# A DiT block on one core: computing the MLP scale on VectorE from transposed weight columns instead of in one TensorE section

## The chip, the cores and the metric

The kernel runs on one NeuronCore of a Trainium2 chip. The metric is the device time of one execution in microseconds (us), taken from repeated executions. A *median* below is over all runs of a kernel in one comparison; each comparison ran the kernel before in turn with the others on the same chip. The records also give the mean clock that TensorE was granted, as a share of full speed.

## The reference

One diffusion transformer block: B = 2 images, N = 256 tokens, D = 1152 channels, two heads, F = 4608 hidden units, all in bfloat16.

```python
mod = (_silu(c) @ w_mod).reshape(B, 6, 1, D)
shift_a, scale_a, gate_a, shift_m, scale_m, gate_m = [mod[:, i] for i in range(6)]
h = _layernorm(x) * (1 + scale_a) + shift_a
q, k, v = ...                       # from h @ wqkv
attn = _softmax(einsum('bqhd,bkhd->bhqk', q, k) * Dh ** -0.5)
a = einsum('bhqk,bkhd->bqhd', attn, v).reshape(B, N, D) @ wo
x = x + gate_a * a
h2 = _layernorm(x) * (1 + scale_m) + shift_m
return x + gate_m * (_gelu(h2 @ w_fc1) @ w_fc2)
```

The change concerns `scale_m`: 1152 numbers for each of two images, from a matrix product with only two rows.

## The kernel before

The activations are kept transposed (channels on partitions), so `scale_m` and `shift_m` are wanted as columns, [128 partitions, 9 chunks, image]. A section is made by 36 narrow matmuls: for each of nine k chunks, four column tiles of the array work on four interleaved quarters of the outputs, and a VectorE 32x32 transpose turns the result into columns.

```python
def vec_section(stat, w, name):                 # 9 x 4 matmuls of 288 columns
    pn = aux_tile([P, CTW], "pn")
    for k in range(KD):
        wk4 = w[:, k, :].rearrange("p (j q r) -> p q j r", q=4, r=32)
        for i in range(4):
            nc.tensor.matmul(pn[32 * i:32 * i + SW, :]..., stat[:, k, :], wk4[:, i, :, :],
                             start=(k == 0), stop=(k == KD - 1), tile_position=(0, 32 * i))
    dst = act.tile([P, KD, 32], FP32, name=name)
    nc.vector.transpose(dst..., pn[:])
    return dst
```

The MLP's gate already goes another way late in the kernel: its weights are loaded transposed, and VectorE multiplies each column block with a broadcast copy of silu(c) and sums along the free axis.

```python
def dot_section(wT, s_all, spill, dst):
    for j in range(KD):
        for b in range(B):
            nc.vector.scalar_tensor_tensor(spill, wT[:, j, :], 1.0, s_all[:, b, :], op0=ALU.mult, op1=ALU.mult,
                                           accum_out=dst[:, b * KD + j:b * KD + j + 1])
```

All weights and the activation transposes are issued by SyncE in program order, into one queue. This is that order in the middle of the kernel:

```python
w_v = load_panels("w_v", wqkv_v, 2 * D)          # 3 x 0.88 MB
load_section("w_gate_a", S_GATE_A, w_gate_a)     # 2.65 MB each
w_o = load_panels("w_o", wo_v, 0)
w_shift_m = load_section("w_shift_m", S_SHIFT_M)
# ... q, scores, softmax; attn_transpose(0), attn_transpose(1); value matmuls, attention gate ...
w_scale_m = load_section("w_scale_m", S_SCALE_M)
w_f1[0] = load_panels("w_f1_0", wfc1_v, 0)
# ... attention product, w_o groups of tiles 0 and 1 with LN2 statistics between ...
ln2_transpose(0)                                 # hT[:, :, tile] <- transposed xn2
# ...
ln2_transpose(1)
# two panels of w_f1_1
shift_m = vec_section(sT, w_shift_m, "shift_m")
scale_m = vec_section(sT, w_scale_m, "scale_m")
# w_o groups of tiles 2 and 3; between them, on ScalarE:
ln2_modulate(0, range(6)); ln2_modulate(0, range(6, KD))    # hT = hT * scale_m + shift_m, nine times
# fc1, first half of the tokens: matmul k needs modulation k
```

## Time and profile before

| | before |
|---|---|
| time, median of 3 runs | 244.07 us (244.01 to 244.39) |
| TensorE busy | 237.0 us of a span of 242.9 us |
| VectorE, ScalarE, GpSimd busy | 84.3, 66.0, 31.4 us |
| hT of the first half landed | 94.27 us |
| TensorE reaches fc1 | 98.72 us, without a gap |

TensorE is the bound, so only its own work and its gaps count. This is the order of time on SyncE in the kernel before (start, length, instruction, x count); the length is how long the issue held SyncE, not the transfer:

```profile
44.25 10.23 SPq L121 DMA_DIRECT2D w_o<-in_wo_dram  x3
54.58 4.64 SPq L115 DMA_DIRECT2D w_shift_m<-in_w_mod_dram  x3
```

By 59 us everything that the attention half needs has been issued, and w_shift_m with it; w_o went out at 44 us.

### The profile page before, as it was taken

What the parts mean: (1) busy time and instruction counts of PE and PEld (TensorE: products, weight loads), DVE (VectorE), ACT (ScalarE), POOL (GpSimd) and SP (SyncE); (2) the same over time, 40 slices, a digit from 0 to 9 for tenths busy, and PEclk for the clock granted to TensorE, in tenths of its full rate; (3) what the DMA queues carried; (4) which work ended last, traced back from release to release, by engine and by line L of the source; (5) the groups of instructions that cost most, each with busy time, mean ns of one, the idle gap of its engine ahead of it and who ended that gap; (6) DMA issues with size and microseconds to landing.
All of it is one profiled execution on the core that took longest, in us unless ns stands there. A gap on an engine that the chain in (4) does not pass through costs nothing.

```text
span 242.9 us, 3965 instructions
## 1 busy us (share of the span) xinstructions
PE 237.0 (98%) x1679; PEld 141.6 (58%) x1679; DVE 84.3 (35%) x195; ACT 66.0 (27%) x131; POOL 31.4 (13%) x47
## 2 busy tenths in 40 slices
PE   8999999999999999999999999999999999999994
PEld 2586444465666676888644444444665665656673
DVE  3762460315634776720000089993010000000001
ACT  6442250333614074774222223332000000000000
POOL 1000004000310515300000000003121111111111
PEclk9999999999999999999999999999999999999999
DMA  6999999999999998699999999996920000000000
GB/s 238 327 333 361 382 349 313 372 354 343 342 185 362 343 217 216 172 186 327 328 336 191 244 305 327 327 326 196 305 81 16 19 16 16 16 26 26 17 19 16
DMA packets 69757, 53.89 MB, mean 222 GB/s; under 512 B 19035, under 2 KB 64363, under 8 KB 69739
## 3 DMA queue, kind: packets, MB, share of 16 engines
q1 hardware_dynamic: 69008, 52.43, 74.8%
q0 software_dynamic: 704, 1.20, 1.7%
q8 instruction: 13, 0.21, 0.4%
q14 instruction: 5, 0.04, 0.1%
q10 hardware_dynamic: 27, 0.00, 0.0%
HBM read 48.08 MB, written 1.19 MB: 203 GB/s over the span
## 4 chain that ended last, share of the span: by engine, by line
PE 86%; SPq 7%; DMA 5%; issue 0%; DVE 0%; DVEq 0%
PE pacc L803 29%; PE pacc L742 29%; PE pacc L644 7%; PE pacc L535 7%; DMA w_shift_a<-in_w_mod_dram 5%; PE pacc L462 5%; SPq L109 4%; PE pacc L470 2%; SPq L115 2%; PE pa L562 1%; PE ps_s L490 1%; PE pn L388 1%; PE pk L298 1%; SPq L104 1%; PE pg L422 0%
## 5 line engine op out<-in xcount | busy, mean ns | idle before, releaser
L803 PE MATMUL pacc<-w_f,gT 128*128 128x384 bf16 (+2 forms) x468 | 70.5, 314 | 0.0
L742 PE MATMUL pacc<-hT,w_f 128*128 128x512 bf16 (+1 forms) x414 | 70.3, 333 | 0.0
L803 PEld LDWEIGHTS <-gT 128*128 128x128 bf16 x468 | 44.4, 98 | 26.3
L742 PEld LDWEIGHTS <-w_f 128*128 128x128 bf16 x414 | 40.5, 98 | 29.4
L453 DVE SCALAR_TENSOR_TENSOR late<-w_gate_mT,late 128x1152 bf16<-128x1152 bf16 x18 | 24.4, 1357 | 31.8 <-DMA w_gate_mT<-in_w_mod_dram 31.2
L809 DVE TENSOR_TENSOR tmp<-pacc,gate 128x384 f32<-128x384 f32 (+2 forms) x13 | 6.9, 527 | 66.9 <-PE pacc L803 54.8
L780 ACT ACTIVATE gT<-pacc 128x512 bf16<-128x512 f32 x26 | 15.5, 597 | 35.0 <-PE pacc L742 35.0
L811 POOL TENSOR_TENSOR o_sb<-tmp,x 128x384 bf16<-128x384 f32 (+1 forms) x12 | 11.7, 972 | 52.2 <-DVE tmp L809 52.2
L644 PE MATMUL pacc<-w_o,big 128*128 128x384 bf16 (+2 forms) x117 | 18.1, 314 | 0.0
L535 PE MATMUL pacc<-w_v,hT 128*128 128x384 bf16 x108 | 17.9, 326 | 0.0
L644 PEld LDWEIGHTS <-big 128*128 128x128 bf16 x117 | 10.9, 98 | 7.1 <-DVE big L286 0.6
L535 PEld LDWEIGHTS <-hT 128*128 128x128 bf16 x108 | 10.4, 98 | 7.2 <-issue 0.5
L269 PE MATMUL pk<-big,w_k 128*128 128x128 bf16 (+2 forms) x102 | 13.4, 278 | 0.0
L650 POOL TENSOR_TENSOR x<-tmp,x_sb 128x384 f32<-128x384 f32 (+1 forms) x11 | 9.8, 889 | 17.0 <-DVE tmp L649 10.6
L462 PE MATMUL pacc<-hT,w_q 128*128 128x512 bf16 x54 | 11.8, 379 | 0.0
L444 POOL DMA_DIRECT2D gates_dram<-grow x4 | 2.0, 513 | 66.3 <-DVE grow L766 66.3
L269 PEld LDWEIGHTS <-w_k 128*128 128x128 bf16 x102 | 7.8, 98 | 2.9
L462 PEld LDWEIGHTS <-w_q 128*128 128x128 bf16 x54 | 5.3, 98 | 6.4
L152 PE MATMUL pwarm<-zeros 128*128 128x512 bf16 x20 | 7.6, 553 | 1.2 <-DVE eps_t L92 1.2
L649 DVE TENSOR_TENSOR tmp<-pacc,gate 128x384 f32<-128x384 f32 (+2 forms) x13 | 6.7, 524 | 5.4 <-PE pacc L644 4.1
L627 ACT ACTIVATE hT<-hT,shift_m,scale_m 128x256 bf16<-128x256 bf16 x12 | 6.2, 587 | 5.0 <-DMA hT<-xn 5.0
L758 ACT ACTIVATE gT<-pacc 128x512 bf16<-128x512 f32 x10 | 5.6, 593 | 6.2 <-PE pacc L742 6.2
(98 smaller groups left out, 155.9 us busy)
## 6 DMA issues: line engine op xcount, KB each, us to landing
w_f<-in_w_fc_dram SPq DMA_DIRECT2D x14, 864.0 KB, 10.1
w_f<-in_w_fc_dram SPq DMA_DIRECT2D x2, 2592.0 KB, 11.9
w_f<-in_w_fc_dram SPq DMA_DIRECT2D x2, 1728.0 KB, 12.2
w_shift_a<-in_w_mod_dram SPq DMA_DIRECT2D x3, 864.0 KB, 11.7
w_v<-in_wqkv_dram SPq DMA_DIRECT2D x3, 864.0 KB, 11.3
w_gate_a<-in_w_mod_dram SPq DMA_DIRECT2D x3, 864.0 KB, 9.8
w_o<-in_wo_dram SPq DMA_DIRECT2D x3, 864.0 KB, 13.3
w_shift_m<-in_w_mod_dram SPq DMA_DIRECT2D x3, 864.0 KB, 9.7
```

What stands on the lines that cost most here:

```text
L109: nc.sync.dma_start(w_k[:, k, 0:KM1 * P], wqkv_v[:, k, D:D + KM1 * P])
L152: nc.tensor.matmul(dst[:], zeros[:, 0:P], zeros[:], start=True, stop=True)
L269: nc.tensor.matmul(pk[m][:, c0:c1], w_k[:, k, m * P:(m + 1) * P], hT0[:, k, c0:c1], start=(k == 0 and c0 == 0), stop=(k == KD - 1), skip_g ...
L453: nc.vector.scalar_tensor_tensor(spill, wT[:, j, :], 1.0, s_all[:, b, :], op0=ALU.mult, op1=ALU.mult, accum_out=dst[:, b * KD + j:b * KD + ...
L462: nc.tensor.matmul(pq[m][:], w_q[:, k, m * P:(m + 1) * P], hT[:, k, :], start=(k == 0), stop=(k == KD - 1),)
L535: nc.tensor.matmul(pacc[:], hT[:, k, t * P:(t + 1) * P], w_v[:, k, pnl * PW:(pnl + 1) * PW], start=(k == 0), stop=(k == KD - 1),)
L644: nc.tensor.matmul(pacc[:], aT[:, k, t * P:(t + 1) * P], w_o[:, k, c0:c1], start=(k == 0), stop=(k == KD - 1),)
L650: (nc.vector if (t, i) in ((1, 2), (3, 3)) else nc.gpsimd).tensor_tensor(x1[:, t, c0:c1], tmp[:], x_sb[:, t, c0:c1], op=ALU.add)
L742: nc.tensor.matmul(dst, w_f1[m // KD][:, k, ml * P:(ml + 1) * P], hT[:, k, c0:c1], start=(k == 0), stop=(k == KD - 1),)
L780: nc.scalar.activation(gT[:, m, :], pacc[:], ACT.Gelu_apprx_tanh)
L803: nc.tensor.matmul(pacc[:], gT[:, kk, t * P:(t + 1) * P], w_f2[j][:, r, c0 - n * PW:c0 - n * PW + cw], start=(kk == 0), stop=(kk == KF - 1),)
L811: (nc.vector if last else nc.gpsimd).tensor_tensor(o_sb[:], tmp[:], x1[:, t, c0:c0 + cw], op=ALU.add)
```

## The change

The intent is to take most of the scale section off TensorE. Two thirds of `scale_m` (six of nine column blocks) are computed by VectorE passes as for the MLP's gate, from weights loaded transposed; the last third by 36 matmuls of 96 columns straight after the attention gate's. For this the broadcast of silu(c) is made earlier, VectorE gives its q and value evictions to ScalarE, and the loads get a new order: the two transposed loads go among the value panels, and **w_o and w_shift_m move behind both attention transposes**.

```diff
@@ loads @@
+    w_scale_m = wide_tile("w_scale_m")
+    w_v = wide_tile("w_v")
     w_gate_a = wide_tile("w_gate_a")
-    w_v = load_panels("w_v", wqkv_v, 2 * D)
-    load_section("w_gate_a", S_GATE_A, w_gate_a)
-    w_o = load_panels("w_o", wo_v, 0)
-    w_shift_m = load_section("w_shift_m", S_SHIFT_M)
+    NDOT = 2 * CPP                                  # CPP = 3 blocks of 128
+    w_scale_mT = w_scale_m[:, 0:NDOT, :]
+    w_scale_mN = w_scale_m[:, NDOT:KD, :]...        # the plain third
+    def load_scale_mT(j):
+        c0 = S_SCALE_M * D + j * P
+        nc.sync.dma_start_transpose(w_scale_mT[:, j:j + CPP, :], w_mod[:, c0:c0 + PW])
@@ gate_natural: 32 weight columns, one eviction on ScalarE @@
-                    pn[32 * i:32 * i + B, :], sT[:, k, 0:B], wg[:, k, i * CTW:(i + 1) * CTW],
+                    pn[32 * i:32 * i + SW, :], sT[:, k, :], wg[:, k, i * CTW:(i + 1) * CTW],
@@ ahead of the q matmuls @@
+    for b in range(B):
+        nc.sync.dma_start(s_b[b][:], s_dram[b:b + 1, :].partition_broadcast(P))
+    load_scale_mT(0)
+    load_v(0)
+    load_section("w_gate_a", S_GATE_A, w_gate_a)
+    nc.sync.dma_start(w_scale_mN, wmod_v[:, :, S_SCALE_M * D + NDOT * P:(S_SCALE_M + 1) * D])
+    load_v(1)
+    load_scale_mT(CPP)
+    load_v(2)
+    scale_m_dots(0, CPP)                            # 6 VectorE passes
@@ q and value evictions @@
-        evac(...)                                   # VectorE and ScalarE in turn
+        nc.scalar.mul(...) / nc.scalar.copy(...)
@@ value loop @@
         if i == 1:
             gate_a = gate_natural(0, w_gate_a)
-
-    w_scale_m = load_section("w_scale_m", S_SCALE_M)
+            scale_mN = vec_section(sT, w_scale_mN, "scale_mN", KD - NDOT)
+        if i == 2:
+            scale_m_dots(CPP, NDOT)                 # 6 VectorE passes
+            ... add 1.0 to both parts
+    w_o = load_panels("w_o", wo_v, 0)
+    w_shift_m = load_section("w_shift_m", S_SHIFT_M)
     w_f1[0] = load_panels("w_f1_0", wfc1_v, 0)
@@ ahead of the third tile's w_o groups @@
     shift_m = vec_section(sT, w_shift_m, "shift_m")
-    scale_m = vec_section(sT, w_scale_m, "scale_m")
```

More of the change, by code (lines that the diff above doesn't have):

```diff
@@ L128, with load_v @@
     nc.sync.dma_start(w_q[:, :, KM1 * P:D], wqkv_v[:, :, KM1 * P:D])
+    w_scale_m = wide_tile("w_scale_m")
+    w_v = wide_tile("w_v")
     w_gate_a = wide_tile("w_gate_a")
-    w_v = load_panels("w_v", wqkv_v, 2 * D)
-    load_section("w_gate_a", S_GATE_A, w_gate_a)
-    w_o = load_panels("w_o", wo_v, 0)
-    w_shift_m = load_section("w_shift_m", S_SHIFT_M)
+    NDOT = 2 * CPP
+    w_scale_mT = w_scale_m[:, 0:NDOT, :]
+    w_scale_mN = w_scale_m[:, NDOT:KD, :].rearrange("p k n -> p (k n)").rearrange("p (k n) -> p k n", k=KD)
+    def load_scale_mT(j):
+        c0 = S_SCALE_M * D + j * P
+        nc.sync.dma_start_transpose(w_scale_mT[:, j:j + CPP, :], w_mod[:, c0:c0 + PW])
+    def load_v(n):
+        nc.sync.dma_start(w_v[:, :, n * PW:(n + 1) * PW], wqkv_v[:, :, 2 * D + n * PW:2 * D + (n + 1) * PW])
     big1 = act.tile([P, 4 * KD, T], BF16, name="big1", tag="big")
@@ L301, in k_panel, with store_by_quadrant @@
             )
+    s_dram = tc.dram_tile([B, D], BF16, name="s_dram")
+    def store_by_quadrant(dst, src, rows):
+        for a in range(4):
+            nc.gpsimd.dma_start(dst[a], src[32 * a:32 * a + rows])
+    s_rows = work.tile([P, KD, SW], BF16, name="s_rows", tag="s_rows", bufs=1)
     CUT = 4 * P
@@ L360 @@
     norm1(3, CUT, D, "d")
+    nc.vector.transpose(s_rows[:].rearrange("p k c -> p (k c)"), sT[:].rearrange("p k c -> p (k c)"))
+    store_by_quadrant(s_dram[:].rearrange("b (k a r) -> a b k r", a=4, r=32), s_rows, B)
     k_step(0, N + P, T)
@@ L381, with vec_section @@
     CTW = D // 4
-    def vec_section(stat, w, name):
-        pn = aux_tile([P, CTW], "pn")
+    def vec_section(stat, w, name, nk=KD):
+        pn = aux_tile([P, nk * 32], "pn")
         for k in range(KD):
@@ L392, in vec_section @@
                 )
-        dst = act.tile([P, KD, 32], FP32, name=name)
+        dst = act.tile([P, nk, 32], FP32, name=name)
         nc.vector.transpose(dst[:].rearrange("p k c -> p (k c)"), pn[:])
@@ L426, in gate_natural @@
         nat = work.tile([P, CTW], BF16, name="nat", tag="nat", bufs=1)
+        nc.scalar.copy(nat[:], pn[:])
         for i in range(4):
             rows = slice(32 * i, 32 * i + B)
-            if i % 2 == 0:
-                nc.vector.tensor_copy(nat[rows, :], pn[rows, :])
-            else:
-                nc.scalar.copy(nat[rows, :], pn[rows, :])
             nc.gpsimd.dma_start(gates_dram[g, :, i * CTW:(i + 1) * CTW], nat[rows, :])
@@ L437, in gate_natural, with dot_passes, scale_m_dots @@
         return gate
-    s_dram = tc.dram_tile([B, D], BF16, name="s_dram")
-    def store_by_quadrant(dst, src, rows):
-        for a in range(4):
-            nc.gpsimd.dma_start(dst[a], src[32 * a:32 * a + rows])
-    s_rows = work.tile([P, KD, SW], BF16, name="s_rows", tag="s_rows", bufs=1)
-    nc.vector.transpose(s_rows[:].rearrange("p k c -> p (k c)"), sT[:].rearrange("p k c -> p (k c)"))
-    store_by_quadrant(s_dram[:].rearrange("b (k a r) -> a b k r", a=4, r=32), s_rows, B)
-    def dot_section(wT, s_all, spill, dst):
-        for j in range(KD):
+    def dot_passes(wT, s_b, spill, dst, js):
+        for j in js:
             for b in range(B):
                 nc.vector.scalar_tensor_tensor(
-                    spill, wT[:, j, :], 1.0, s_all[:, b, :], op0=ALU.mult, op1=ALU.mult,
-                    accum_out=dst[:, b * KD + j:b * KD + j + 1],
-                )
-    gate_a = None
+                    spill, wT[:, j, :], 1.0, s_b[b], op0=ALU.mult, op1=ALU.mult, accum_out=dst(j, b),
+                )
+    s_b = [work.tile([P, D], BF16, name="s_b", tag="xn", bufs=4) for _ in range(B)]
+    s_spill = work.tile([P, D], BF16, name="s_spill", tag="xn", bufs=4)
+    for b in range(B):
[7 more added lines that the diff above has]
+    load_v(2)
+    scale_m = act.tile([P, KD, B], FP32, name="scale_m")
+    def scale_m_dots(j0, j1):
+        dot_passes(
+            w_scale_mT, [t[:] for t in s_b], s_spill[:], lambda j, b: scale_m[:, j, b:b + 1], range(j0, j1),
+        )
+    scale_m_dots(0, CPP)
     pq = [acc_tile([P, T], "pacc") for _ in range(KM1)]
@@ L473 @@
                 )
-        evac(qT[:, m, :], pq[m][:], attn_scale)
+        nc.scalar.mul(qT[:, m, :], pq[m][:], attn_scale)
     n_s = B * H * TPB
@@ L538, in v_group @@
             )
-        evac(v_sb[:, t, pnl * PW:(pnl + 1) * PW], pacc[:])
+        nc.scalar.copy(v_sb[:, t, pnl * PW:(pnl + 1) * PW], pacc[:])
     gate_a = None
@@ L550 @@
             gate_a = gate_natural(0, w_gate_a)
-    w_scale_m = load_section("w_scale_m", S_SCALE_M)
+            scale_mN = vec_section(sT, w_scale_mN, "scale_mN", KD - NDOT)
+        if i == 2:
+            scale_m_dots(CPP, NDOT)
+            nc.vector.tensor_scalar_add(scale_m[:, 0:NDOT, :], scale_m[:, 0:NDOT, :], 1.0)
+            nc.vector.tensor_scalar_add(scale_m[:, NDOT:KD, :], scale_mN[:, :, 0:B], 1.0)
+    w_o = load_panels("w_o", wo_v, 0)
+    w_shift_m = load_section("w_shift_m", S_SHIFT_M)
     w_f1 = [None] * 4
@@ L619, in ln2_transpose @@
         nc.sync.dma_start_transpose(hT[:, :, t * P:(t + 1) * P], xn2[t][:])
-    shift_m = scale_m = None
     def ln2_modulate(b, ks=range(KD)):
@@ L683 @@
     shift_m = vec_section(sT, w_shift_m, "shift_m")
-    scale_m = vec_section(sT, w_scale_m, "scale_m")
-    nc.vector.tensor_scalar_add(scale_m[:, :, 0:B], scale_m[:, :, 0:B], 1.0)
     wo_group(2, 0)
@@ L781 @@
         if m == 14:
-            dot_section(w_gate_mT, s_all, late[:, B, :], gcol)
+            dot_passes(
+                w_gate_mT, [s_all[:, b, :] for b in range(B)], late[:, B, :],
+                lambda j, b: gcol[:, b * KD + j:b * KD + j + 1], range(KD),
+            )
             gate_m = gate_m_finish()
```

## The prediction

> **What bounds the kernel now.** I read the page's shares, then the chain that ended last, then the order of time on each engine around the two places that the change touches (36 to 80 us and 86 to 100 us), then the DMA rates in short windows.
>
> ```profile
> PE 237.0 (98%) x1679; PEld 141.6 (58%) x1679; DVE 84.3 (35%) x195; ACT 66.0 (27%) x131; POOL 31.4 (13%) x47
> PE 86%; SPq 7%; DMA 5%; issue 0%; DVE 0%; DVEq 0%
> ```
>
> TensorE is busy 98% of the span, and the chain of waits runs over it without a break from 31.4 us to 239.3 us. So only two things move the time: TensorE work taken away, and new gaps. What is taken away is the scale section behind the second attention product:
>
> ```profile
> 87.59 1.29 PE L388 MATMUL pn<-w_shift_m,sT 128*32 128x288 bf16 x36
> 88.70 1.28 PE L388 MATMUL pn<-w_scale_m,sT 128*32 128x288 bf16 x36
> 89.91 8.97 PE L644 MATMUL pacc<-w_o,big 128*128 128x384 bf16 x63
> 98.72 1.47 PE L742 MATMUL pacc<-hT,w_f 128*128 128x256 bf16 x12
> ```
>
> The columns are start, length, instruction and count. One section costs 88.70 - 87.59 = 1.11 us of TensorE, 30.8 ns per matmul (four column tiles run together). Its second limit is near: fc1 starts at 98.72 us on activations that ScalarE is still modulating.
>
> ```profile
> 94.27 3.06 ACT L627 ACTIVATE hT<-hT,shift_m,scale_m 128x256 bf16<-128x256 bf16 x6 [3.42 <-DMA hT<-xn]
> 97.30 0.29 ACT L600 ACTIVATE rstd<-mv,eps_t 128x1 f32<-128x1 f32 x1
> 97.50 1.57 ACT L627 ACTIVATE hT<-hT,shift_m,scale_m 128x256 bf16<-128x256 bf16 x3
> ```
>
> The bracket says that ScalarE waited 3.42 us for the transposed hT to land at 94.27. The nine modulations end at 99.07; the ninth matmul of fc1 needs the last at 98.72 + 8 x 0.11 = 99.6 (180 such matmuls take 19.8 us). **This chain (normalise, DMA transpose, modulate, fc1) has only 0.5 us of slack.** The transposes stand in SyncE's queue behind the weight loads:
>
> ```profile
> 60.49 8.59 SPq L522 DMA_TRANSPOSE attnT_all<-soft  x2
> 69.17 1.60 SPq L115 DMA_DIRECT2D w_scale_m<-in_w_mod_dram  x3
> 70.87 10.88 SPq L121 DMA_DIRECT2D w_f<-in_w_fc_dram  x3
> 87.29 4.86 SPq L619 DMA_TRANSPOSE hT<-xn  x2
> ```
>
> and these are the DMA rates there (last two columns: DMA share and GB/s; before them the engines' busy times):
>
> ```profile
> 72.00:74.00 2.00, 2.00 (x14) 1.19 (x13) 0.56 (x1) 0.11 (x1) 1.05 (x2) 1.00 1.02 370
> 80.00:82.00 2.00, 2.00 (x14) 1.17 (x12) 1.46 (x3) 0.00 (x0) 1.32 (x2) 1.00 1.10 351
> ...
> 88.00:90.00 2.00, 2.00 (x69) 1.56 (x58) 0.81 (x5) 1.46 (x5) 0.00 (x0) 1.00 0.98 127
> 90.00:92.00 2.00, 2.00 (x13) 1.19 (x14) 1.64 (x5) 0.85 (x1) 0.00 (x0) 1.00 0.27 60
> ```
>
> The backlog of weights ends at about 88.3 us, just as the first hT transpose is issued; both transposes land in 3.3 and 3.6 us because the queue is empty.
>
> **What the Trainium skill says.** "TensorE: Matmul & The Clock Gate", section "Back-to-back issue gap": up to 64 columns cost about 60 cycles, a floor near 25 ns; above that N/2.4 + 2.5 ns. The trace agrees: 27 matmuls of 2 columns take 0.82 us with their last 0.16 us, (0.82 - 0.16)/26 = 25 ns; and 288 columns, (120 + 2.5)/4 = 30.6 ns, against 30.8 measured. "DMA: Bandwidth & Descriptors", "Queues, rings and completion order": on each DMA engine descriptors are consumed in ring order, so a short transfer waits behind what was issued before. The trace agrees: the attention transpose issued at 60.49 behind w_shift_m took 10.4 us to land, the next one, behind no weights, 4.6 us. "Advanced Engine Details and Errata", "X-Bar Transpose (TRN2)": transposing DMAs are as fast as regular ones. This trace does not agree: while w_gate_m is loaded transposed the windows show 190 and 212 GB/s, against 326 for plain fc1 weights in 116 to 122 us. I take the measurement. I found no page that gives the accumulate pass of VectorE a duration; the trace has it.
>
> **The change part by part.**
>
> 1. TensorE loses 36 matmuls of 288 columns at 88.7 us: -1.11 us. It gains 36 of 96 columns (nine k, four column tiles, a third of the outputs) after the attention gate at about 59.7 us. By columns that would be 0.37 us, but the issue floor holds: 36 x 25 = 0.9 us (estimate from the pm row), at most 1.11. **Net gain 0 to 0.2 us.** The gate's matmuls now load 32 columns of weights instead of 2; their 288 moving columns set the pace, so nothing.
>
> 2. VectorE gains 12 passes of 128x1152. The same pass in the kernel before takes 1357 ns, start to start 1.40 us: two blocks of six, 8.4 us each. The first stands ahead of the softmax (VectorE idle from 36.7 to 44.9, apart from evictions that move to ScalarE). It needs the first transposed load. Before, w_q landed at 38.8 us and the next load 1.3 us later; adding two s broadcasts (0.59 MB, 1.7 us) and 0.88 MB at about 200 GB/s (4.3 us), I put that landing at 43 to 45 us, the block's end at 52 to 54, and softmax starts at 55.4: hidden by 1 to 3 us, with 1.7 us more before the value matmuls want their buffers. The second block follows softmax at about 65.9 and ends at 74.4, just before VectorE's eviction of the attention product at 75: hidden. VectorE loses four q and six v evictions; ScalarE has room for them (q: 0.60 us each against 1.97 us per nine matmuls).
>
> 3. Loads. The bytes are the same plus 0.59 MB; two thirds of one section go at 200 instead of 340 GB/s, 2 x 1.8 = 3.6 us more. The last v panel should land at about 65 us, wanted at 68.5. But **w_o and w_shift_m now stand behind the attention transposes**, and the second waits for the last softmax (about 65.9, issue 2.1 us). w_o is issued at 68 us where it was 44. First panel at about 73, wanted at 77.7: in time. w_shift_m at 86, wanted at 88.5: in time. Behind them fc1's first section: w_o + w_shift_m + w_f1_0 = 7.96 MB, with 0.59 MB of gate broadcasts 8.55 MB, at 350 GB/s (my mean of 72 to 88 us) 24.4 us from 69.3: done at 93.7 instead of 88.3.
>
> 4. The LN2 chain. The hT transposes are issued at 88.3 and 91.9 (1 us later, by part 1) into a queue that is busy to 93.7. The first lands 2.6 us after the backlog ends, as before (88.3 to 90.9), the second about 1 us after it: 97.3 instead of 94.3. Modulation ends at 97.3 + 4.8 = 102.1. TensorE wants it at 99.6 - 1.11 + 0.95 = 99.4. **A new stall of about 2.7 us.**
>
> Sum: 244.07 - 0.2 + 2.7 = 246.6. Since part 3 and 4 rest on a byte count with some 2 us of play, I say 246.2.
>
> **Rivals.** (a) *No queueing*: the transposes overlap the fc1 load or it finishes sooner. Then the chain is still 0.95 us later (the new section precedes it) against 0.5 us of slack, and TensorE reaches fc1 0.2 us earlier: about +0.4 us, 244.5. For it speaks that completion is not strictly in order: w_v's first panel landed 1.3 us after w_q's last although 2.5 us of bytes lay between. (b) *The transposed load is late*: its rows here are 768 bytes, those of w_gate_m 2304. If each takes 9 us, the first block ends near 58 us, softmax and then the value matmuls stall 2 to 4 us, and the last v panel lands at 73 instead of 68.5: 249 to 252. Against it: the order of the loads leaves 3 us everywhere by my count. (c) *TensorE gains the full column saving*, 0.7 us, and nothing stalls: 243.4. Against it the 25 ns floor and the 0.5 us slack. (d) w_shift_a, which TensorE already waits for at 31.4, is delayed by the earlier store of s: 4 x 1.1 KB, so under 0.3 us.
>
> **Range and chances.** (c) sets the floor, (a) the lower edge, parts 3 and 4 the middle, (b) the upper tail. I weigh the queueing at 60%, (a) and (c) at 28%, (b) at 12%. Range 243.9 to 248.8. Over 2% faster (below 239.2) has no source: 1%. Over 2% slower (above 249.0) needs (b) or a longer backlog: 9%.
>
> **What will show it.** Part 1: the 96-column section takes 0.9 to 1.1 us, not 0.4. Part 2: the first block starts at 43 to 45 us, ends before the first maximum, whose start stays near 55.4. Part 3: w_o issued near 68, fc1's first section landing near 94, GB/s above 300 through 92 us. Part 4: ScalarE's first modulation starts near 97 and waits on the hT transpose for 5 to 6 us; TensorE shows a gap of 2 to 3 us ahead of fc1 that ends on ScalarE. I am wrong if that gap is under 1 us, if TensorE is idle between 55 and 76 us, or if fc1 starts before 99 us.

## The result, and the profile after

| | before | after |
|---|---|---|
| median of 6 runs each | 244.26 us (244.01 to 244.39) | 247.81 us (246.36 to 249.32) |
| ratio | | 1.0145, 95% interval 1.0103 to 1.0188 |
| profiled run: time, span, granted clock | span 242.9, 1.0 | 248.65, span 246.9, 0.993 |

A ratio is the mean time of one kernel's fast runs over the mean of the other's fast runs of the same rounds, so it is not quite the ratio of the medians. The change costs about 1.5%.

The page of the changed kernel, its shares, the chain that ended last, and the clock by slices:

```profile
PE 238.5 (97%) x1670; PEld 141.9 (57%) x1679; DVE 93.3 (38%) x207; ACT 70.9 (29%) x141; POOL 31.3 (13%) x47
PE 57%; ACT 2%; DMA 2%; SPq 1%; issue 1%; DVE 0%; ACTq 0%; DVEq 0%
PEclk9999999999999999799999999999999999999999
```

Three things differ from before. TensorE was given less work and yet is busy 1.5 us longer. The chain that ended last used to run over TensorE without a break from 31 us to the end of fc2; now it is followed back from fc1 through ScalarE and a DMA (so PE has only 57% of it). And the clock row has a 7: in that slice, 99 to 105 us, TensorE got only some 70% of its clock.

The order of time on TensorE (start, length, instruction, count, and in brackets the idle time before it with what ended it):

```profile
58.50 1.29 PE L440 MATMUL pg<-w_gate_a,sT 128*32 128x288 bf16 x36
59.61 0.56 PE L406 MATMUL pn<-w_scale_m,sT 128*32 128x96 bf16 x36
60.10 14.80 PE L557 MATMUL pacc<-w_v,hT 128*128 128x384 bf16 x90
...
98.17 0.63 PE L767 MATMUL pacc<-hT,w_f 128*128 128x256 bf16 x2
99.03 0.27 PE L767 MATMUL pacc<-hT,w_f 128*128 128x256 bf16 x1 [0.22 <-ACT hT L654]
...
102.16 12.09 PE L767 MATMUL pacc<-hT,w_f 128*128 128x256 bf16 x95 [0.22 <-ACT hT L654]
```

The same place in the kernel before, where the value matmuls follow the gate directly:

```profile
58.51 1.27 PE L422 MATMUL pg<-w_gate_a,sT 128*2 128x288 bf16 x36
59.72 14.80 PE L535 MATMUL pacc<-w_v,hT 128*128 128x384 bf16 x90
```

From the gate's first matmul to the value matmuls is now 60.10 - 58.50 = 1.60 us, where it was 59.72 - 58.51 = 1.21. The new section thus costs 0.39 us (the 60.10 - 59.61 = 0.49 us from its start contain 0.1 us of changing to another shape of matmul, which came after the gate before). The old one cost 1.11, so TensorE gains 0.72 us. Some 0.18 of it is lost again in w_o's first 54 matmuls (9.18 us from start to end instead of 9.00), and TensorE reaches fc1 at 98.17 instead of 98.72. There it runs into ScalarE: each of the first matmuls waits for one modulation. The ninth starts at 102.16 instead of 99.6. Without the wait it would have started at 98.17 + 8 x 0.11 = 99.05, so the gap is 3.1 us.

The order of time on ScalarE for the same stretch:

```profile
97.39 3.06 ACT L654 ACTIVATE hT<-hT,shift_m,scale_m 128x256 bf16<-128x256 bf16 x6 [5.99 <-DMA hT<-xn]
```

And the piece of the chain that ended last just before it (start, length, what):

```profile
93.44 3.85 DMA hT<-xn
```

ScalarE waited 5.99 us (3.42 before) for the second hT transpose, which landed at 97.3. Behind which transfers it stood is on SyncE:

```profile
33.19 8.07 SPq L138 DMA_TRANSPOSE w_scale_m<-in_w_mod_dram  x1
...
48.95 11.45 SPq L138 DMA_TRANSPOSE w_scale_m<-in_w_mod_dram  x1
61.13 5.75 SPq L544 DMA_TRANSPOSE attnT_all<-soft  x2
66.97 3.32 SPq L121 DMA_DIRECT2D w_o<-in_wo_dram  x3
...
77.53 10.03 SPq L121 DMA_DIRECT2D w_f<-in_w_fc_dram  x3
87.85 7.62 SPq L647 DMA_TRANSPOSE hT<-xn  x2
```

w_o went out at 66.97 us, not at 44.25, and the DMA windows (last two columns: DMA share and GB/s) show when the weights behind it were through:

```profile
90.00:92.00 2.00, 2.00 (x15) 1.20 (x13) 1.65 (x5) 0.92 (x1) 0.24 (x1) 1.00 1.11 328
92.00:94.00 2.00, 2.00 (x14) 1.22 (x13) 1.06 (x3) 0.00 (x0) 1.53 (x2) 1.00 1.92 261
```

In the kernel before, 90 to 92 us moved at 60 GB/s: the queue was empty. Here it is full until about 93.

The clock needs shorter windows (the first number after the length is TensorE's busy time; the third from the end is its granted clock):

```profile
99.00:99.50 0.50, 0.27 (x1) 0.10 (x1) 0.00 (x0) 0.50 (x2) 0.00 (x0) 1.00 1.09 359
...
102.00:102.50 0.50, 0.34 (x2) 0.25 (x2) 0.50 (x2) 0.50 (x2) 0.22 (x2) 0.50 1.10 326
...
105.00:106.00 1.00, 1.00 (x9) 0.81 (x8) 0.00 (x0) 0.98 (x2) 0.00 (x0) 0.80 1.08 203
```

From 98.5 to 102.0 TensorE worked 0.27 us of each 0.50. At 102.0, just as the data came, its clock fell to half, and it came back in 105 to 106 us.

The profiled runs add up: the ninth fc1 matmul is 102.16 - 99.6 = 2.56 us later; from there to the start of fc2 it is 71.0 us instead of 69.44 (173.16 - 102.16 against 169.04 - 99.6), 1.56 us lost to the clock; the rest is 0.12 us shorter. 2.56 + 1.56 - 0.12 = 4.0 = 246.9 - 242.9.

### The profile page after: what moved, and what is told of

It is laid out like the page before. It is cut to its first block, busy times and chain, and to the rows that moved or that the text cites. A ratio compares the mean times of both kernels' runs of the same rounds, so it can differ in the third digit from the quotient of the medians.

```text
span 246.9 us, 3983 instructions
## 1 busy us (share of the span) xinstructions
PE 238.5 (97%) x1670; PEld 141.9 (57%) x1679; DVE 93.3 (38%) x207; ACT 70.9 (29%) x141; POOL 31.3 (13%) x47
## 4 chain that ended last, share of the span: by engine, by line
PE 57%; ACT 2%; DMA 2%; SPq 1%; issue 1%; DVE 0%; ACTq 0%; DVEq 0%
PE pacc L767 29%; PE pacc L831 28%; ACT hT L654 2%; DMA hT<-xn 2%; SPq L647 1%; ACT xn L637 0%; ACT rstd L628 0%; DVE tmp L837 0%; DVE o_sb L839 0%; ACTq L654 0%; DVEq L837 0%
## 5 line engine op out<-in xcount | busy, mean ns | idle before, releaser
L767 PE MATMUL pacc<-hT,w_f 128*128 128x512 bf16 (+1 forms) x409 | 72.9, 338 | 2.1 <-ACT hT L654 1.7
L767 PEld LDWEIGHTS <-w_f 128*128 128x128 bf16 x414 | 41.2, 100 | 33.4 <-issue 3.2
L458 DVE SCALAR_TENSOR_TENSOR late<-w_gate_mT,late 128x1152 bf16<-128x1152 bf16 x18 | 24.4, 1357 | 32.3 <-DMA w_gate_mT<-in_w_mod_dram 31.7
L458 DVE SCALAR_TENSOR_TENSOR s_spill<-w_scale_m,s_b 128x1152 bf16<-128x1152 bf16 x12 | 16.3, 1358 | 8.9 <-DMA w_scale_m<-in_w_mod_dram 8.6
L496 ACT ACTIVATE big<-pacc 128x512 bf16<-128x512 f32 x9 | 4.8, 609 | 12.3 <-PE pacc L484 9.6
```

The lines of the kernel that those rows point to most:

```text
L458: nc.vector.scalar_tensor_tensor(spill, wT[:, j, :], 1.0, s_b[b], op0=ALU.mult, op1=ALU.mult, accum_out=dst(j, b),)
L767: nc.tensor.matmul(dst, w_f1[m // KD][:, k, ml * P:(ml + 1) * P], hT[:, k, c0:c1], start=(k == 0), stop=(k == KD - 1),)
```

## The experiments

The first question was why hT lands late. **Theory A**: what counts is how many bytes of weights stand ahead of the hT transposes in the one queue; w_o was moved behind the attention transposes, so more is left when hT is issued. **Theory B**: the two transposed loads are slow and alone push everything back. **Theory C**, formed after the second run: each is enough by itself to leave the queue full, so undoing one shows nothing. The second question is whether the lost clock belongs to the gap. Each experiment's kernel before, run in turn on the same chip, had its median at 244.29 (e1 to e4), 244.39 (e5 to e8) and 244.50 us (e9 to e11).

### e1: the fc1 panels spread around the hT transposes

```diff
-    w_f1[0] = load_panels("w_f1_0", wfc1_v, 0)
+    load_f1_0(0)                       # one of three panels
     ln2_transpose(0)
+    load_f1_0(1)
     ln2_transpose(1)
+    load_f1_0(2)
```

> The changed kernel with one thing moved: of the first fc1 section only one panel is loaded ahead of the first hT transpose, the second panel between the two transposes, the third behind them. Theory A (the short hT transposes queue behind w_o, w_shift_m and the whole fc1 section, and TensorE waits for them, then runs at a lower clock): the second transpose lands near 94 instead of 97.4, the gap ahead of fc1 goes, the clock stays 1.0, and the time is 243.4 to 243.9. Theory B (the time went into the slow transposed loads, the VectorE passes or ScalarE's evictions): still above 246.5.

Measured: 249.02 us (247.9 to 249.54), ratio 1.0192 (1.0167 to 1.0216). Slower, not faster. The order of time on SyncE in this run:

```profile
87.83 1.28 SPq L652 DMA_TRANSPOSE hT<-xn  x1
89.16 0.68 SPq L585 DMA_DIRECT2D w_f<-in_w_fc_dram  x1
91.41 3.08 SPq L652 DMA_TRANSPOSE hT<-xn  x1
```

The piece of its chain that follows the second transpose:

```profile
91.41 6.01 DMA hT<-xn
```

And its DMA windows:

```profile
90.00:92.00 2.00, 2.00 (x15) 1.22 (x13) 1.63 (x5) 0.92 (x1) 0.26 (x1) 1.00 1.41 87
92.00:94.00 2.00, 2.00 (x14) 1.22 (x13) 1.09 (x3) 0.00 (x0) 1.54 (x2) 1.00 1.10 309
```

The queue did empty before the transposes, as theory A wants. But the panel between them, issued at 89.16 behind the first transpose, hardly moved until that was done (87 GB/s in 90 to 92), then ran at 309 GB/s in front of the second, which again landed at 97.4. The edit put a new obstacle where the old one had been. What follows: the miss does not refute A, and transposes and plain loads serialise in the order of the queue. Panels should go behind a pair of transposes, not between them; e11 below does that.

### e2: plain loads instead of the transposed ones

```diff
-        nc.sync.dma_start_transpose(w_scale_mT[:, j:j + CPP, :], w_mod[:, c0:c0 + PW])
+        nc.sync.dma_start(<the same tile viewed as p k n>, wmod_v[:, :, c0:c0 + PW])
```

The result is wrong (relative error 0.044): VectorE multiplies untransposed weights. All work keeps its size.

> The changed kernel with its two transposed loads of the MLP scale replaced by plain loads of the same bytes in the same places (the result is wrong on purpose). Theory A, in its form that w_o's place behind the attention transposes makes the backlog: w_o is still issued at 66 to 68, hT lands within 1 us of before the edit, time 247 to 248.5. Theory B (the slow transposed loads make the backlog): everything behind them moves up by 4 us or more, 244 to 245.

Measured: 250.92 us (249.16 to 251.44), ratio 1.0272 (1.0253 to 1.0291). The transposed loads gone, the time rose. The order of time on SyncE:

```profile
66.73 7.43 SPq L121 DMA_DIRECT2D w_o<-in_wo_dram  x3
```

A DMA window just ahead of it:

```profile
64.00:66.00 2.00, 2.00 (x14) 1.19 (x13) 1.40 (x4) 1.75 (x7) 0.87 (x2) 1.00 0.03 2
```

And the order of time on TensorE:

```profile
79.71 1.64 PE L674 MATMUL pacc<-w_o,big 128*128 128x384 bf16 x9 [1.04 <-DMA w_o<-in_wo_dram]
```

The loads were through early: the DMA engines stood dry (2 GB/s in 64 to 66 us). Yet w_o was issued at 66.73 as before, because the second attention transpose waits for the last softmax, and SyncE issues in order. Time saved ahead of that wait is thrown away at it. So theory B alone falls. Theory A's own forecast for this run, 247 to 248.5 us with hT landing within 1 us of the changed kernel, missed as well: hT landed at 99.3, 2 us later, the ninth fc1 matmul started at 104.20, and the run has the two waits for w_o besides. Why w_o then took 9.6 to 14.0 us to land, longer than with the slow loads in front (TensorE waited 1.04 us for its second panel and another 1.01 us for its third), these runs do not settle.

### e3: the kernel before with more ahead of the hT transposes

```diff
+    <two panels of w_f1_1, 1.77 MB>
     ln2_transpose(0)
     ...
     ln2_transpose(1)
-    <two panels of w_f1_1>
```

> The kernel before with two panels (1.77 MB) of the second fc1 section loaded ahead of the hT transposes instead of behind them; nothing else. Theory A: the backlog ends near 93.4 instead of 88.3, the second transpose lands near 97 instead of 94.3, TensorE gets a gap of about 2 us ahead of fc1 and its clock falls after it: 246 to 248. Theory B: no change, 244.0 to 244.6.

Measured: 246.56 us (246.31 to 248.5), ratio 1.0111 (1.0076 to 1.0146). ScalarE of this run:

```profile
96.94 3.06 ACT L627 ACTIVATE hT<-hT,shift_m,scale_m 128x256 bf16<-128x256 bf16 x6 [6.08 <-DMA hT<-xn]
```

Moving two loads, and nothing else, turned the wait of 3.42 us into 6.08, moved the ninth fc1 matmul from 99.6 to 101.71 us and cost 2.3 us. This is theory A shown on the other kernel: bytes ahead of the hT transposes alone make most of the loss. The lowered clock that I had forecast did not come in its profile (1.0), and of its four runs only the one of 248.5 us has it (0.990).

### e4: TensorE kept busy through the gap

```diff
     for k in range(KD):
         f1_mm(pacc[:, m - m0, :], m, k, b * N, (b + 1) * N)
+        if b == 0 and m == 0 and k < KD - 1:
+            warm(2, pfill)             # two dummy matmuls of 512 columns
```

> The changed kernel with two dummy 512-column matmuls on zeros after each of the first eight matmuls of fc1, that is in the gap where TensorE waits for ScalarE. If the granted clock falls because TensorE idles there, the clock stays 1.0 and the time falls by 1 to 1.6 us although the wait stays: 246.2 to 246.8, with less spread. If the clock falls for another reason: 247.5 or more, since the fillers can only cost.

Measured: 247.85 us (247.47 to 248.22), ratio 1.0147 (1.0128 to 1.0165). In its profile the clock stayed at 1.0, and from the ninth matmul (102.52 us) to fc2 took 69.44 us, as in the kernel before. The 1.56 us came back in that run. But the median did not fall: the fillers made the ninth matmul 0.36 us late, and this run waited 0.55 us for w_o. One of four runs had a lowered clock, against four of six of the changed kernel, which is too few to tell. By the rule that I had set (247.5 us or more) the run came out against the idea; the profile alone speaks for it. The three runs at full clock (247.47, 247.77 and 247.93 us) lie about 1.2 us above the two of the changed kernel (246.36 and 246.68), so the fillers cost nearly what they might have saved. That they keep the clock is not shown.

### e5 and e6: w_o between the two attention transposes, with plain and with transposed scale loads

```diff
             if j % H == H - 1:
                 attn_transpose(j // H)
+            if j == H - 1:
+                w_o = load_panels("w_o", wo_v, 0)
 ...
-    w_o = load_panels("w_o", wo_v, 0)
```

e5 has e2's edit as well (again a wrong result); e6 keeps the transposed loads.

> Both suspects undone at once: plain loads in place of the transposed ones (wrong result on purpose) and w_o's three panels issued between the two attention transposes instead of behind the second. Theory C (either the slow transposed loads or w_o's place behind the last softmax is enough to fill the queue until 93, so that taking away one alone gives nothing): w_o moves in the hole that the plain loads left at 62 to 66 us, the backlog ends near 89, hT lands near 95, and the time is 243.8 to 245. If the cause is neither: above 247.

> The changed kernel with w_o's three panels issued between the two attention transposes; the transposed loads stay. Theory C: the queue is full of transposed and plain weights until 66 anyway, so w_o gains 2 us at most, and the second attention transpose, now behind w_o, lands near 78 and costs TensorE 1 to 2 us at 77: 246 to 249. Theory A with w_o's place alone as the cause: 243.8 to 245.

Measured: e5 244.69 us (243.85 to 245.07), ratio 1.0008 (0.9987 to 1.0029): the whole loss is gone. e6 250.42 us (248.39 to 251.91), ratio 1.0242 (1.0198 to 1.0286): worse than the change. The order of time on TensorE in e6:

```profile
82.35 0.64 PE L607 MATMUL pa<-attnT_all,big 128*64 128x256 bf16 x4 [5.81 <-DMA attnT_all<-soft]
```

And a window inside that wait, in which TensorE did nothing and its clock fell:

```profile
80.00:82.00 2.00, 0.00 (x0) 0.00 (x0) 0.00 (x0) 0.00 (x0) 0.00 (x0) 0.55 0.64 79
```

In e5 w_o went out at 62.39 us, the backlog was through by 90, hT came at 95.38 at the latest and the ninth matmul started at 100.15. With e2, this is half of theory C: with plain loads but a late w_o the queue is full, with plain loads and an earlier w_o it is not. (A gap of some 1.8 us ahead of fc1 was left in e5, and the ninth matmul was still 0.55 us later than in the kernel before.) In e6 the same move put 2.65 MB in front of the second attention transpose while the slow loads still ran late; it took 15.0 us to land, and TensorE stood for 5.81 us. I had expected 1 to 2 us of wait and 246 to 249 us in all; it was the queue's order again, at another place. The other half of theory C, that slow loads with an early w_o also leave the queue full ahead of hT, is not shown by e6: when its hT transposes were wanted the queue was empty (13 GB/s in 98 to 100 us, and ScalarE waited 3.42 us, as in the kernel before).

### e8, e11 and e7: a shorter chain, a shorter queue, and both

e8 leaves the loads alone and moves three of the first half's nine modulations to VectorE:

```diff
-    ln2_modulate(0, range(6, KD))          # ScalarE
...
+    ln2_modulate_d(0, range(6, KD))        # the same on VectorE, after ln2_stats(3, 0)
```

e11 leaves the modulations alone and moves fc1 panels behind the transposes, but behind both of a pair (e1's lesson):

```diff
-    w_f1[0] = load_panels("w_f1_0", wfc1_v, 0)
+    load_f1_0(0); load_f1_0(1)
     ln2_transpose(0) ... ln2_transpose(1)
-    <two panels of w_f1_1>
+    load_f1_0(2); <first panel of w_f1_1>
     ln2_transpose(2) ... ln2_transpose(3)
-    <last panel of w_f1_1>
+    <second and third panel of w_f1_1>
```

e7 has both edits.

> The changed kernel with three of the nine modulations of the first half given to VectorE. Nothing changes in the loads. If TensorE's gap is the landing of hT plus ScalarE's nine modulations, the gap shortens by the three: fc1's ninth matmul starts near 100.9 instead of 102.2, and the time is 246 to 247 (1.2 us less, and a shorter gap may cost less clock). If the gap is something else: as the changed kernel, 247.5 or more.

> An attempt at a version that beats both: the changed kernel with the three modulations on VectorE, the third panel of fc1's first section behind the first two hT transposes, and the second and third panel of its second section behind the last two. The backlog should end near 90.3, hT land near 95, no gap ahead of fc1, clock 1.0: 243.4 to 244.2. If panels then come late, a wait shows on the third panel (at 104) or on the last hT transposes (at 108): up to 246.

> The changed kernel with only the new order of the fc1 panels (less weight ahead of the hT transposes), modulations left on ScalarE. The queue theory says that hT lands at about 95.9 us instead of 97.4, so that the ninth matmul of fc1 starts at 100.7 instead of 102.2 and the time is 245.3 to 246.5. If the order of these panels is worth nothing by itself (the backlog only moves), hT lands within 0.5 us of 97.4 and the time stays at 247.4 to 248.2.

| | median (range), us | ratio (95%) | first modulation, us | fc1 unbroken from, us |
|---|---|---|---|---|
| changed kernel | 247.81 (246.36 to 249.32) | 1.0145 (1.0103 to 1.0188) | 97.39 | 102.16 |
| e8, modulation | 246.03 (245.16 to 246.62) | 1.0065 (1.0044 to 1.0087) | 96.82 | 99.92 |
| e11, order | 245.92 (245.1 to 246.68) | 1.0055 (1.0028 to 1.0083) | 96.04 | 100.81 |
| e7, both | 244.29 (243.36 to 245.02) | 0.9992 (0.9971 to 1.0012) | 95.91 | 99.02 |

The last column is the start of the stretch of fc1 that runs on without a wait. Against the median of the kernel before in its own rounds the changed kernel stands at +3.55 us, e8 at +1.64, e11 at +1.42 and e7 at -0.10. So the modulation takes off 1.9 us (1.8 by the bare medians, as it stands in a later expectation), the order 2.1 and the two together 3.65. e8 and e11 fell in the ranges expected of them; e7, just above its range of 243.4 to 244.2, takes the loss away and ties with the kernel before, no more. These sizes contain the clock: it was lowered (below 0.997) in four of six runs of the changed kernel, two of four of e8, two of six of e11 and one of six of e7. The means of the other runs are 246.5, 245.5, 245.6 and 244.0 us, so at full clock the modulation takes off 1.0 us, the order 0.9 and both 2.5; the rest is fewer runs with a lowered clock, of which there are too few to say how many the edit prevents. The gap is the sum of a late landing and a chain of nine modulations behind it, and either may be shortened. The order of time on TensorE in e11 shows what is left there, a wait for w_o and a shorter one for ScalarE:

```profile
80.42 6.02 PE L677 MATMUL pacc<-w_o,big 128*128 128x384 bf16 x36 [0.31 <-DMA w_o<-in_wo_dram]
100.81 2.45 PE L774 MATMUL pacc<-hT,w_f 128*128 128x256 bf16 x21 [0.22 <-ACT hT L660]
```

### e9: e8's edit on the kernel before

The edit is e8's, on the kernel that has no gap.

> Control for the modulation edit: the kernel before, with three of the nine first-half modulations on VectorE. In the kernel before the ninth matmul of fc1 starts at 99.6 us, where it would start without any wait, within 0.1 us. If the gain of that edit on the changed kernel (1.8 us) came from shortening a gap ahead of fc1, there is no gap here to shorten: 243.9 to 244.6 us, within 0.3 us of the kernel before. If the edit is worth something by itself (ScalarE relieved), the time falls by over 0.5 us as well.

Measured: 244.56 us (244.29 to 245.35), ratio 1.0008 (0.9982 to 1.0034). As expected: ScalarE relieved is worth nothing where TensorE does not wait for it. What e8 gained was the gap.

### e10: e7 with one panel of w_o between the attention transposes

```diff
             if j % H == H - 1:
                 attn_transpose(j // H)
+            if j == H - 1:
+                <first panel of w_o>        # 0.88 MB
 ...
-    w_o = load_panels("w_o", wo_v, 0)
+    <second and third panel of w_o>
```

> The version that tied with the kernel before, with the first panel of w_o (0.88 MB) between the two attention transposes and the other two behind the second. If what is left over the pure TensorE gain of 0.62 us is the wait for w_o (0.40 us at 80.3 and 0.22 us at 99.0 in the version before this) then w_o lands in time and the median is 243.4 to 244.0. The rival: one panel in front already holds the second attention transpose past 76.3 us, where TensorE wants it; then a wait shows there and the time is 244.5 to 246.

Measured: 243.50 us (243.32 to 244.04), against 244.50 us of the kernel before in the same rounds (243.84 to 245.5); ratio 0.996 (0.9934 to 0.9986). It is the fastest version and correct, though by 0.4% only. The order of time on SyncE in this run:

```profile
63.65 0.53 SPq L572 DMA_DIRECT2D w_o<-in_wo_dram  x1
65.28 1.75 SPq L544 DMA_TRANSPOSE attnT_all<-soft  x1
```

Its TensorE at the start of fc1, with no bracket and so no wait:

```profile
97.56 5.66 PE L785 MATMUL pacc<-hT,w_f 128*128 128x256 bf16 x50
```

And two of its DMA windows:

```profile
66.00:68.00 2.00, 2.00 (x14) 1.18 (x13) 1.93 (x5) 0.74 (x2) 0.00 (x0) 1.00 1.14 326
90.00:92.00 2.00, 2.00 (x14) 1.18 (x12) 1.18 (x4) 0.79 (x1) 0.85 (x1) 1.00 1.32 67
```

One panel is small enough not to hold the second transpose (no wait at 76 us), and it fills a stretch in which the changed kernel moved 182 GB/s. The queue is empty again by 90 us (67 GB/s), hT's first modulation starts at 94.42, and fc1 starts at 97.56 without a gap. Here at last the gain of TensorE shows: fc1 starts 0.99 us earlier than in e9 (98.55), the kernel before with e8's edit. Some 0.72 us of that is the section, and 0.22 is there before it: the gate's matmuls start at 58.12 instead of 58.34. The cause of that step was not followed up.

## Why the prediction was right or wrong

I predicted 246.2 us in a range of 243.9 to 248.8; it became 247.81. The mechanism was right, its size was short.

**Part 1, the floor of 25 ns per matmul: wrong.** It put the new section at 0.9 to 1.1 us; it cost 0.39 (0.49 with the change of shape behind it). The net gain of TensorE is thus 0.7 us, not 0 to 0.2. I took the floor from one section of the skill's page and from the two-column matmuls of one tile; matmuls in four column tiles overlap. "TensorE: Matmul & The Clock Gate", section "Measured speedup vs the span model", gives a packed group the length of one matmul plus about 4 ns for each further tile. This trace agrees in the step within a group, 3 to 4 ns. What counts here is how fast the groups follow each other: the nine groups start 42.5 ns apart, 10.6 ns per matmul. The prediction's own working for the old section, (120 + 2.5) / 4 = 30.6 ns, gives just that for a third of the columns: (40 + 2.5) / 4 = 10.6 ns. It set the floor in place of its own formula. The rival (c), the full column saving, was right about TensorE's work and wrong about the end.

**Part 2, VectorE hidden: right.** The first block of passes started at 44.91 us (43 to 45 predicted) and the first softmax maximum at 55.35, where it was 55.37 before. Rival (b), a stalled softmax, did not happen, although the first transposed load kept SyncE for 8.07 us and the second for 11.45.

**Part 3, the queue: right in its course, wrong at one edge.** w_o was issued at 66.97 (68 predicted) and the backlog ended at about 93 (93.7). "In time" was too kind for w_o: the last panel landed at 80.4, just as it was wanted, with waits between 0.06 us in the profiled run and 0.55 in e4. e10, which differs from e7 only in moving a panel of it, stands at -1.00 us where e7 stands at -0.10. In their profiles 0.56 us of that lies in the stretch of w_o's matmuls (8.94 us instead of 9.50) and 0.46 in the last of the gap ahead of fc1, as hT comes earlier too.

**Part 4, the chain: right.** ScalarE's first modulation was put at 97.3 and came at 97.39; the stall was put at 2.7 us and was 3.1. That is no second error: part 1 let TensorE arrive too late, and it only waited longer. Net gain and stall together, -0.2 + 2.7 = 2.5 us, stand against the 2.56 us by which the ninth matmul moved. Rival (a), no queueing, was wrong, and e3, e5 and e11 show why: less or more ahead of the transposes moves their landing. One of the prediction's signs of being wrong, fc1 starting before 99 us, came true by the letter: the first of its matmuls ran at 98.17. The sign was badly put, since by the prediction's own sum TensorE would be there at 98.72 - 1.11 + 0.95 = 98.56; the run without waits began at 102.16.

**What the sum lacked: the clock.** It stood at 246.6 before rounding down. The two runs of the changed kernel whose clock stayed at 0.997 or above are 246.36 and 246.68 us. The four others, at 0.984 to 0.993, took 247.73 to 249.32. In the profiled one the loss is 1.56 us and follows the gap. "TensorE: Matmul & The Clock Gate", section "What's actually happening", says that the clock is halved after an idle window of about 3.4 us that runs free of the program, and restored after a busy one. Here it was halved from 102.0 to about 105.4 us (0.50 up to 105, 0.80 in 105 to 106), which agrees in size and length; but TensorE had not been idle before it, only busy for 54% of 3.5 us. The profile of e1 shows the same after its gap, e6's during its own; e4 with a filled gap and e8 with a shorter one kept the clock in their profiles. But so did e2, e3 and e11, with gaps that nothing filled, so a gap alone doesn't do it. The profiles speak for the free-running window: in the changed kernel the half clock lasted from 101.98 to 105.39 us, in e1 from 102.96 to 106.38, 3.41 us each, and all stretches at full clock between two changes are whole multiples of 3.41 us. Laid out on that grid, the window just before the fall held seven fc1 matmuls of 0.11 us in the changed kernel (about 22% of it), eleven in e1 (about 34%) and none in e6; the windows at the gaps of e3 and e11, which kept the clock, held fourteen and fifteen (about 45%). So in the profiled runs the clock fell after a window of the grid with little work, and a gap of like size that lay otherwise against the grid did not bring it down. How little is enough is not measured more closely, and of the other runs only the mean clock is recorded. Nor is the gap its only source: the kernel before has lowered clocks too, in 5 of its 31 runs of the experiments (0.993, about 1 us slower than the others), and where in those runs is not recorded.

What stays open: why w_o landed so late in e2, and where the kernel before loses clock in some of its runs.

## What to carry to other kernels

A saving on the busiest engine is worth nothing if the loads that it needs are taken from in front of something the same engine waits for: before you count it, list everything in that queue with the time of its issue, and look for a transfer that cannot start until a computation is done, because all that is behind it moves too. Undo one suspect at a time and then both, since here the plain loads alone and the early w_o alone each made it worse and together they removed the loss. Where a chain of small steps stands between a late transfer and the bound, shortening the chain on an idle engine (1.9 us here) may buy about as much as mending the queue (2.1 us); about half of each was clock.

## What the Trainium skill lacked or had wrong

- "TensorE: Matmul & The Clock Gate", "Wait — 56ns, not 53.3ns?" (and the same floor in "Back-to-back issue gap"): "Start-to-start never drops below ≈25 ns however small N is". It should say that this holds within one tile of the array. The two-column matmuls of one tile started every 25 ns, but 96-column ones over four column tiles 3 to 4 ns apart, four in every 42.5 ns. The section on packing has the span of one group, not how fast groups follow each other.
- The same page, "What's actually happening": it speaks of idle and busy windows, and "A second HAM failure mode: psum-queue depth-cycling" of frequent short idle times that make the clock swing; neither says how busy a window must be. Here 3.5 us at 54% busy, with no single wait over 0.41 us in it, were followed by 3.41 us at half clock (1.56 us lost), where the last 3.41 us before the fall held about 22% of matmul work; windows with about 45% kept the clock in e3 and e11; in 4 of 6 runs of the changed kernel the mean clock was lowered.
- "Advanced Engine Details and Errata", "X-Bar Transpose (TRN2)": transposes as fast as plain loads. "DMA: Bandwidth & Descriptors", "Latency and other measured facts", has a lower figure for some layouts (261 GB/s). Here the mean rate over 38 to 44 us was 188 GB/s in the changed kernel, whose first transposed load runs there, and 338 in e2, which has plain loads in its place.
- "DMA: Bandwidth & Descriptors", "Queues, rings and completion order": it lacks that a plain load behind a transpose hardly moves until the transpose is through (87 GB/s for 2 us in e1, then 309).
- No page that I found has how long the issue of a large transposed load holds SyncE: 8.07 and 11.45 us for 0.88 MB, against 0.5 to 0.7 us for a plain panel of that size where the queue had room. The two lengths contain any wait for room in the queue, which the profile does not separate.
- No page that I found has VectorE's multiply pass with a sum along the row: 1357 ns for 128x1152 in bfloat16, 1.40 us from start to start.
